# Shift-convolution taps: summed by accumulating transfers within SBUF instead of by matmuls

## The chip, the core and the metric

The kernel runs on one core of a Trainium2 chip. The metric is device time in microseconds of one execution; lower is better. The engines are PE (matrix products, with its weight loads shown as PEld), DVE and ACT (elementwise work), POOL (a slow elementwise engine that also issues DMAs) and SP (issues DMAs only). Data lies in HBM, in SBUF (128 partitions) and, for results of PE, in PSUM, which PE writes and DVE and ACT read.

## The reference

The sequence has S = 2048 positions and D = 640 channels, and all arrays are bf16. Two branches are mixed by a gate that is computed per position.

```python
# branch A: short convolution of k (4 taps), times v, then a long convolution by FFT
k_pad = jnp.pad(k, ((0, 0), (ks - 1, 0), (0, 0)))
for t in range(ks):                       # ks = 4
    k_shift = k_shift + k_pad[:, t:t + S, :] * shift_k[:, ks - 1 - t][None, None, :]
kv = k_shift * v
y = irfft(rfft(pad(kv)) * rfft(pad(ssm_k)))[:, :S, :]   # along the sequence
y = y + kv * ssm_D
a = q * y
# branch B: a two-layer MLP along the sequence
h = layernorm(x)                          # x is q
u = gelu(einsum("bsd,sf->bdf", h, w1) + b1)             # F = 1536
b = transpose(einsum("bdf,fs->bds", u, w2) + b2)
out = g * a + (1 - g) * b                 # g = sigmoid(sum(x * gate_w))
```

Only the loop over the four taps and the product with v are touched by the change.

## The kernel before

**Branch A.** The sequence is cut into P = 4 parts of 512 positions, and each part into NB = 4 tiles of 128 positions, so that there are 16 k tiles. `kv_load` loads a tile into `k4` (128 x 4 x 640: for each position the row itself and the three rows before it, 640 KB) and its v into `v_` (160 KB). There are four k4 buffers and five v buffers. `kv_tile` multiplies k4 by the broadcast tap weights `shkb` on DVE (one instruction of 2560 elements). It then sums the four products on PE: four matmuls with the identity (for the first two tiles of a part) or with a flip matrix that reverses the 128 positions (for the other two) are accumulated in PSUM, each in two halves of 320 columns, since a bank of PSUM holds no more. ACT copies the sum into a row of `kvb`, and DVE multiplies it by v. For the flipped tiles, v is turned first, by two more matmuls and a copy on ACT.

When the four tiles of a part are there, `a_split` forms sums and differences `es` of the halves of `kvb` (DVE), `a_freq` transforms them into the spectrum `A{j}` by matmuls with tables (PE, then copies on ACT). The filter goes through the same steps into `W{i}`, with sums and differences between neighbouring parts (`w_comb`). `pair(j, m)` multiplies A{j} with W{m-j} and adds it to `Z{m}`, on DVE; there are ten pairs and two Z buffers. `inverse(m)` transforms Z back on PE, and `epilogue(m)` turns half of the result with flip matmuls, multiplies by q, adds the MLP's output and stores.

**Branch B.** DVE computes the layernorm into `h` (bn_stats, then one instruction per tile). The first layer is 384 matmuls `pp<-h,w`, whose weights come in w1 loads, mostly issued by POOL; the second is 384 matmuls `pp<-gT,w`, whose weights come in w2 loads by POOL. ACT applies the gelu and moves the second layer's results to `o1`.

**What sets the order.** While the program is built, `_Plan.run` puts all operations in an order by a list schedule. Each has a cost, a priority `pr` (lower goes first) and predecessors by the tiles that it reads and writes; its rank is the longest chain that follows it. A DMA takes its engine 0.5 us (SP) or 1.2 us (POOL), and then its bytes at `DMA_RATE` 0.30 MB/us on one common pipe, and 2.0 us more. This gives one fixed order per engine, and the engines then run in that order and wait on semaphores. So an instruction that waits holds up all that is behind it on its engine, and this holds for the DMAs that SP and POOL issue too.

**Names in the profile.** All matmuls have line L290, all of DVE's two-operand products L676, all ACT operations L718, and all DMA issues L258; so groups are told apart by their tiles. `k<-k,shkb` is the tap product, `pp<-k,ident` and `pp<-k,flip` are the matmuls that sum the taps, `kvb<-kvb,v` is the product with v, `pp<-v,flip` turns v, `es<-kvb` is the split, `tT<-A,W`, `Z<-A,W` and `Z<-Z,tT` are the pairs, `W<-W,W` is w_comb, `W<-W` are small copies within SBUF issued by SP, `xg<-xg,gwb` is the gate's product and `pp<-Z,TI` the inverse.

Of the kernel before, what the change touches and what calls it, by code (L numbers as in the profile page):

```python
# [11 lines left out]
ACT = mybir.ActivationFunctionType  # L12
ALU = mybir.AluOpType
# [4 lines left out]
class _Tracker:  # L18
# [227 lines left out]
    def dma(self, stream, out_ap, in_ap, semname, noncontig=False, accum=False):  # L246
        reads = [in_ap]
        writes = [out_ap]
        acc = self.pre(stream, reads, writes)
        engobj = self.eng[stream]  # L250
        sem = self.dma_sems[semname]
        if accum:
            ins = engobj.dma_start(out_ap, in_ap, accum_op=ALU.add)
        elif noncontig:
            with self.nc.allow_non_contiguous_dma(reason="tiny"):
                ins = engobj.dma_start(out_ap, in_ap)
        else:
            ins = engobj.dma_start(out_ap, in_ap)  # L258
        ins.then_inc(sem, 16)
        self.dma_cnt[semname] += 16  # L260
        v = self.dma_cnt[semname]
        self.dma_hist[(semname, v)] = dict(self.known[stream])
        src = ("dma", semname, v)
        for reg, mode in acc:
            self.add_record(reg, mode, src)
        return v
# [250 lines left out]
def _build(nc, A_q, A_k, A_v, A_shift_k, A_ssm_k, A_ssm_D, B_x, B_w1, B_b1, B_w2, B_b2, gate_w, out):  # L517
    Bsz, S, D = A_q.shape
    F = B_w1.shape[1]
    KS = A_shift_k.shape[1]  # L520
# [4 lines left out]
    NB = n // 128  # L525
# [7 lines left out]
    with ExitStack() as es:  # L533
# [3 lines left out]
        T = _Tracker(nc, clk)  # L537
# [5 lines left out]
        plan = _Plan(T, 4)  # L543
# [61 lines left out]
        KR = 4  # L605
# [3 lines left out]
        KVB = 1  # L609
# [31 lines left out]
        for name, shape, dtype, t0, t1 in spec:  # L641
            size = mybir.dt.size(dtype)
# [19 lines left out]
        def vop(eng, cost, f, reads, writes, pr, ps=(), after=()):  # L662
            def emit():
                rr = [a() if callable(a) else a for a in reads]
                T.op(eng, f, rr, writes)
            return plan.add(eng, cost, emit, [a for a in reads if not callable(a)], writes, pr, ps=ps, after=after)

        def nel(ap):
            k = 1
            for st, ct in list(ap.ap)[1:]:  # L670
                k *= ct
            return k

        def tt(out_, in0, in1, op, pr, eng="DVE"):
            c = 0.07 + nel(out_) / 1920.0 if eng == "DVE" else 0.3 + nel(out_) / 500.0
            return vop(eng, c, lambda e: e.tensor_tensor(out_, in0, in1, op), [in0, in1], [out_], pr)  # L676
# [19 lines left out]
        def act(out_, in_, func, pr, bias=None, scale=None, accum=None, ps=(), after=()):  # L696
            kw = {}
            rr = [in_]
            k = 0
            if bias is not None:  # L700
                kw["bias"] = bias
                if isinstance(bias, bass.AP):
                    rr.append(bias)
                    k += 1
            if scale is not None:
                kw["scale"] = scale
                if isinstance(scale, bass.AP):
                    rr.append(scale)
                    k += 1
            ww = [out_]  # L710
            if accum is not None:
                kw["accum_out"] = accum
                ww.append(accum)
            c = 0.17 + nel(out_) / 1150.0 + 0.09 * k + (0.2 if accum is not None else 0)

            def f(e):
                src = in_() if callable(in_) else in_
                return e.activation(out_, src, func, **kw)  # L718

            return vop("ACT", c, f, rr, ww, pr, ps=ps, after=after)  # L720

        def dma(out_ap, in_ap, semname, pr, stream="SP", noncontig=False):
            if semname not in T.dma_sems:
                T.add_dma_sem(semname, es.enter_context(nc.semaphore(f"d_{semname}")))
            tot = mybir.dt.size(out_ap.dtype)
            for st, ct in list(out_ap.ap):
                tot *= ct

            def emit():
                T.dma(stream, out_ap, in_ap, semname, noncontig=noncontig)  # L730

            return plan.add(stream, 1.2 if stream == "POOL" else 0.5, emit, [in_ap], [out_ap], pr, dma=max(tot, 20000) / 1e6)

        def pe(pslist, mms, pr, after=()):
            reads = []
            for (p_, c0, w_, lhsT, rhs, st, sp) in mms:
                reads.append(lhsT)
                reads.append(rhs)
            cost = sum(0.016 + m[2] * 0.000372 for m in mms)

            def emit():
                full = [(pp[p_.slot][:, c0:c0 + w_], lhsT, rhs, st, sp) for (p_, c0, w_, lhsT, rhs, st, sp) in mms]
                T.mm_part(full)

            return plan.add("PE", cost, emit, reads, [], pr, ps=pslist, after=after)

        def two(p_):
            return lambda: pp[p_.slot][:, :].rearrange("p (c f) -> p c f", c=2)[:, :, 0:HD]
# [4 lines left out]
        def h2(ap):  # L753
            return ap.rearrange("p (c f) -> p c f", c=2)

        b = bufs
# [94 lines left out]
        def dram(t, off, ap):  # L851
            return bass.AP(tensor=t.tensor, offset=t.offset + off, ap=ap)

        dma(b["gwb"][:, :], dram(gate_w, 0, [[0, 128], [1, D]]), "gw", 2.3)

        def rows(t, q):
            return dram(t, q * 256 * D, [[D, 128], [128 * D, 2], [1, D]])

        def w1_load(s_, pr):
            for hf in range(2):  # L860
                nm = f"w1_{(2 * s_ + hf) % 3}"
                step = 4 if s_ == 0 else 8
                for t0 in range(0, 8, step):
                    dma(b[nm][:, t0:t0 + step, :],
                        dram(B_w1, (8 * hf + t0) * 128 * F + s_ * FSET * 128, [[F, 128], [128 * F, step], [1, FSET * 128]]),
                        f"{nm}_{t0}" if s_ < 1 else f"{nm}_p", pr + 0.35 * (8 * hf + t0), stream="SP" if s_ < 1 else "POOL")
# [4 lines left out]
        def wnat_load(i, pr):  # L871
            dma(b[f"wnat{i}"][:, :, :], dram(A_ssm_k, i * n, [[S, 128], [128 * S, DC], [1, n]]),
                f"wnat{i}", pr)
# [10 lines left out]
        for gi, g in enumerate(groups):  # L884
            xs = b[f"xs{g[0] // 8}"][:, g[0] % 8:g[-1] % 8 + 1, :]
            gn = len(g)
            pr = 1.0 + g[0] * 0.08
# [19 lines left out]
        def halves(p_, pairs, st=True, sp=True):  # L907
            k = len(pairs)
            res = []
            for c in range(2):  # L910
                for i, (l_, r_) in enumerate(pairs):
                    res.append((p_, c * 512, HD, l_, r_[:, c * HD:(c + 1) * HD], st and i == 0, sp and i == k - 1))
            return res
# [3 lines left out]
        p_ = _PS()  # L917
# [4 lines left out]
        for j in range(KS):  # L922
            p_ = _PS()
# [63 lines left out]
        for s_ in range(1, NSET):  # L987
            w1_load(s_, 2.5 if s_ < 2 else 6.0 + 2 * s_)
            for fi in range(FSET):
                p_ = _PS(True)  # L990
# [36 lines left out]
        def kv_tile(t, pr):  # L1027
            k4 = b[f"k4_{t % KR}"]
            v_ = b[f"v_{t % VR}"][:, :]
            r_ = t % NB  # L1030
            mat = b["ident" if r_ < 2 else "flip"][:, :]
            kb = b[f"kvb{t // NB % KVB}"][:, r_ if r_ < 2 else 5 - r_, :]
            if r_ >= 2:
                p_ = _PS()
                pe([p_], halves(p_, [(mat, v_)]), 1.1)
                act(h2(v_), two(p_), ACT.Copy, 1, ps=[p_])
            tt(k4[:, :, :], k4[:, :, :], b["shkb"][:, :, :], ALU.mult, pr)
            p_ = _PS()
            pe([p_], halves(p_, [(mat, k4[:, j, :]) for j in range(KS)]), 1.1)
            act(h2(kb), two(p_), ACT.Copy, 1, ps=[p_])  # L1040
            tt(kb, kb, v_, ALU.mult, pr - 2)

        def a_freq(j, pr):
            A = b[f"A{j}"]
# [9 lines left out]
        def kv_two(i):  # L1054
            for t in range(NB * i, NB * i + NB):
                kv_load(t, 8.0 + t)
                kv_tile(t, 11.0 + 0.5 * t)
# [176 lines left out]
```

## Time and profile before

| what | value |
|---|---|
| median of three timed runs | 226.09 us (223.95 to 227.66) |
| span of the profiled execution | 222.4 us (the profile gives no other time for it) |
| PE busy | 202.8 us, of it the tap sums 18.7 us |
| DVE busy | 201.8 us, of it the tap products 23.4 us |
| ACT busy | 139.9 us |
| POOL busy | 41.5 us |
| DMA | 39.88 MB, mean 179 GB/s |

The span runs from the first to the last instruction. Busy time is the sum of an engine's instructions, without waits. In a group's line, the number after x is how many instructions there are, then follow their busy time in us and the mean ns of one, and then the time for which the engine was idle just before them, with what ended most of it. In a line of the timeline, the first number is the start in us, the second the duration, and the bracket the idle time before it. Matmuls overlap, so that a group's busy time is less than count times mean.

### The profile page before, as it was taken

Reading aid. Unit: us, or ns where it says so; the run is one execution under the profiler, and the core shown is the slowest. Engines: PE = TensorE matmul, PEld = TensorE weight load, DVE = VectorE, ACT = ScalarE, POOL = GpSimd, SP = SyncE. Lnnn points to the kernel's source line nnn. Section 1 sums busy time; section 2 is a strip of 40 time slices with the busy share of each in tenths; the row PEclk is TensorE's granted clock in tenths of the full one; section 3 lists DMA queues with packets and bytes.
Section 4 is the critical chain, followed back from the end, with each engine's and each line's share of the span. In section 5 each row is a group of like instructions: output and inputs, shape, how many; then the busy total and the mean of one; then the engine's idle time right before and its main releaser. Section 6 shows DMA issues by size and latency. Waiting matters only on the chain.

```text
span 222.4 us, 3751 instructions
## 1 busy us (share of the span) xinstructions
PE 202.8 (91%) x1481; PEld 141.1 (63%) x1481; DVE 201.8 (91%) x253; ACT 139.9 (63%) x221; POOL 41.5 (19%) x79
## 2 busy tenths in 40 slices
PE   0829799999998998999999999999999999999991
PEld 0725547567675774777777777667777777767651
DVE  3379999899988998999999999999999999999771
ACT  4899988997579869683746511799431845432251
POOL 8563330301131010015171010000101101110000
PEclk9988999999999999999999999999999999999997
DMA  6999996139915894899962114302065845286003
GB/s 180 359 325 349 235 298 244 43 109 304 347 41 146 297 391 160 287 295 294 288 181 58 36 16 140 119 3 59 0 202 169 244 116 180 83 253 200 0 3 118
DMA packets 22087, 39.88 MB, mean 179 GB/s; under 512 B 1715, under 2 KB 17205, under 8 KB 22069
## 3 DMA queue, kind: packets, MB, share of 16 engines
q1 hardware_dynamic: 18964, 28.10, 39.8%
q0 software_dynamic: 3104, 11.54, 17.9%
q8 instruction: 12, 0.20, 0.4%
q14 instruction: 7, 0.05, 0.1%
HBM read 36.35 MB, written 2.62 MB: 175 GB/s over the span
## 4 chain that ended last, share of the span: by engine, by line
PE 60%; DVE 22%; ACT 11%; DMA 5%; issue 1%; DVEq 0%; SPq 0%
PE pp L290 60%; DVE Z L676 10%; DVE tT L676 7%; DMA k<-in_A_k_dram 3%; ACT wT L718 2%; ACT W L718 2%; DMA wnat<-in_A_ssm_k_dram 2%; ACT L718 1%; DVE es L676 1%; DVE cg L676 1%; ACT kvb L718 1%; DVE kvb L676 1%; DVE k L676 1%; DVE xg L676 1%; ACT TFs L718 1%
## 5 line engine op out<-in xcount | busy, mean ns | idle before, releaser
L290 PE MATMUL pp<-h,w 128*128 128x320 bf16 x384 | 54.9, 299 | 0.0
L290 PE MATMUL pp<-gT,w 128*128 128x320 bf16 x384 | 53.1, 299 | 0.0
L676 DVE TENSOR_TENSOR tT<-A,W 128x640 bf16<-128x640 bf16 (+4 forms) x44 | 48.0, 1121 | 0.3
L676 DVE TENSOR_TENSOR Z<-Z,tT 128x2560 bf16<-128x2560 bf16 (+3 forms) x35 | 47.1, 1370 | 0.1
L290 PEld LDWEIGHTS pp<-gT,w 128*128 128x128 bf16 x384 | 37.5, 98 | 14.8 <-issue 0.3
L290 PEld LDWEIGHTS pp<-h,w 128*128 128x128 bf16 x384 | 37.5, 98 | 14.6
L258 POOL DMA_DIRECT2D w<-in_B_w_dram x18 | 17.3, 962 | 117.7 <-PE pp L290 117.1
L718 ACT ACTIVATE o<-pp,c,omg 128x640 bf16<-128x640 f32 x16 | 14.2, 884 | 31.4 <-PE pp L290 31.4
L676 DVE TENSOR_TENSOR k<-k,shkb 128x2560 bf16<-128x2560 bf16 x16 | 23.4, 1485 | 0.6 <-DMA k<-in_A_k_dram 0.5
L718 ACT ACTIVATE A<-pp 128x640 bf16<-128x640 f32 x32 | 20.0, 717 | 2.0 <-PE pp L290 2.0
L718 ACT ACTIVATE gT<-pp,bf 128x640 bf16<-128x640 f32 x12 | 9.5, 792 | 18.3 <-PE pp L290 18.2
L290 PE MATMUL pp<-Z,TI 128*128 128x320 bf16 x128 | 18.4, 299 | 1.1 <-ACT kvb L718 1.1
L718 ACT ACTIVATE W<-pp 128x640 bf16<-128x640 f32 x24 | 15.9, 707 | 3.9 <-PE pp L290 3.8
L290 PE MATMUL pp<-ident,wnat 128*128 128x128 bf16 x80 | 8.0, 274 | 10.1 <-DMA wnat<-in_A_ssm_k_dram 5.4
L290 PEld LDWEIGHTS pp<-Z,TI 128*128 128x128 bf16 x128 | 12.4, 98 | 6.4 <-ACT kvb L718 1.4
L718 ACT ACTIVATE kvb<-pp 128x640 bf16<-128x640 f32 x16 | 11.2, 701 | 5.8 <-PE pp L290 5.8
L290 PEld LDWEIGHTS pp<-ident,wnat 128*128 128x128 bf16 x80 | 6.6, 124 | 11.2 <-DMA wnat<-in_A_ssm_k_dram 5.8
L893 DVE BATCH_NORM_STATS2 stats<-xs 128x6 f32<-128x320 bf16 x32 | 13.3, 475 | 0.0
L718 ACT ACTIVATE xg<-xg 128x640 bf16<-128x640 bf16 x16 | 11.6, 734 | 1.7 <-DVE xg L676 1.7
L676 DVE TENSOR_TENSOR Z<-A,W 128x5120 bf16<-128x5120 bf16 x4 | 11.3, 2819 | 0.7 <-ACT A L718 0.7
L290 PE MATMUL pp<-wT,TFc 128*128 128x320 bf16 x48 | 10.1, 300 | 1.7 <-ACT W L718 1.7
L290 PE MATMUL pp<-es,AFs 128*128 128x320 bf16 x64 | 10.1, 300 | 0.8 <-ACT gT L718 0.8
(92 smaller groups left out, 279.2 us busy)
## 6 DMA issues: line engine op xcount, KB each, us to landing
k<-in_A_k_dram SPq DMA_DIRECT2D x15, 640.0 KB, 7.7
w<-in_B_w_dram POOLq DMA_DIRECT2D x8, 768.0 KB, 5.8
w<-in_B_w_dram POOLq DMA_DIRECT2D x10, 512.0 KB, 6.1
wnat<-in_A_ssm_k_dram SPq DMA_DIRECT2D x4, 640.0 KB, 6.5
v<-in_A_v_dram SPq DMA_DIRECT2D x16, 160.0 KB, 7.4
xg<-in_A_q_dram SPq DMA_DIRECT2D x8, 320.0 KB, 7.1
xe<-in_A_q_dram SPq DMA_DIRECT2D x8, 320.0 KB, 3.1
out_dram<-cg SPq DMA_DIRECT2D x8, 320.0 KB, 4.3
```

Of the source, the lines that this page charges most:

```text
L258: ins = engobj.dma_start(out_ap, in_ap)
L290: ins = self.nc.tensor.matmul(ps_ap, lhsT=lhsT, rhs=rhs, start=start, stop=stop)
L676: return vop(eng, c, lambda e: e.tensor_tensor(out_, in0, in1, op), [in0, in1], [out_], pr)
L718: return e.activation(out_, src, func, **kw)
L893: vop("DVE", 0.41, (lambda o_, i_: lambda e: e.bn_stats(o_, i_))(o_, i_), [i_], [o_], pr)
```

## The change

The four tap products are no longer summed on PE. Two DMAs within SBUF, issued by POOL, add to what lies at their destination: the first adds the products of taps 2 and 3 to those of taps 0 and 1 (128 rows of 1280 elements, 320 KB), the second adds the second half of that sum to the first (640 elements, 160 KB). Both have the same semaphore, and the second waits for the first. DVE multiplies the sum by v. For the first two tiles of a part this product goes straight to `kvb`; for the other two it goes to the v buffer, is turned by two flip matmuls, and is copied to `kvb` by ACT. So v itself is no longer turned. In the planner, an accumulating DMA counts 2.5 times its bytes. The DMA call caps one row of a transfer at 2560 bytes.

```diff
         if accum:
-            ins = engobj.dma_start(out_ap, in_ap, accum_op=ALU.add)
+            ins = engobj.dma_start(out_ap, in_ap, accum_op=ALU.add, max_dma_last_dim=2560)
...
-        def dma(out_ap, in_ap, semname, pr, stream="SP", noncontig=False):
+        def dma(out_ap, in_ap, semname, pr, stream="SP", noncontig=False, accum=False):
...
-                T.dma(stream, out_ap, in_ap, semname, noncontig=noncontig)
-
-            return plan.add(stream, 1.2 if stream == "POOL" else 0.5, emit, [in_ap], [out_ap], pr, dma=max(tot, 20000) / 1e6)
+                T.dma(stream, out_ap, in_ap, semname, noncontig=noncontig, accum=accum)
+
+            size = max(tot, 20000) / 1e6 * (2.5 if accum else 1.0)
+            return plan.add(stream, 1.2 if stream == "POOL" else 0.5, emit, [in_ap], [out_ap], pr, dma=size)
...
-            mat = b["ident" if r_ < 2 else "flip"][:, :]
-            kb = b[f"kvb{t // NB % KVB}"][:, r_ if r_ < 2 else 5 - r_, :]
-            if r_ >= 2:
+            tt(k4[:, :, :], k4[:, :, :], b["shkb"][:, :, :], ALU.mult, pr)
+            nm = f"ka_{t % KR}"
+            dma(k4[:, 0:2, :].rearrange("p j d -> p (j d)"), k4[:, 2:4, :].rearrange("p j d -> p (j d)"),
+                nm, pr, stream="POOL", accum=True)
+            dma(k4[:, 0, :], k4[:, 1, :], nm, pr, stream="POOL", accum=True)
+            if r_ < 2:
+                tt(b[f"kvb{t // NB % KVB}"][:, r_, :], k4[:, 0, :], v_, ALU.mult, pr - 2)
+            else:
+                kb = b[f"kvb{t // NB % KVB}"][:, 5 - r_, :]
+                tt(v_, k4[:, 0, :], v_, ALU.mult, pr - 2)
                 p_ = _PS()
-                pe([p_], halves(p_, [(mat, v_)]), 1.1)
-                act(h2(v_), two(p_), ACT.Copy, 1, ps=[p_])
-            tt(k4[:, :, :], k4[:, :, :], b["shkb"][:, :, :], ALU.mult, pr)
-            p_ = _PS()
-            pe([p_], halves(p_, [(mat, k4[:, j, :]) for j in range(KS)]), 1.1)
-            act(h2(kb), two(p_), ACT.Copy, 1, ps=[p_])
-            tt(kb, kb, v_, ALU.mult, pr - 2)
+                pe([p_], halves(p_, [(b["flip"][:, :], v_)]), 1.1)
+                act(h2(kb), two(p_), ACT.Copy, 1, ps=[p_])
```

## The prediction

> **What bounds the kernel now.** I read the busy times first.
>
> ```profile
> PE 202.8 (91%) x1481; PEld 141.1 (63%) x1481; DVE 201.8 (91%) x253; ACT 139.9 (63%) x221; POOL 41.5 (19%) x79
> ```
>
> Two engines are level: PE at 202.8 us and DVE at 201.8 us of a span of 222.4 us. The chain that ended last gives PE 60% and DVE 22%, but a chain names only one of two engines that are never idle. So the stretches of 20 us (columns: sum, then PE, PEld, DVE, ACT, POOL busy, clock, DMA share, GB/s):
>
> ```profile
> 0.00:20.00 20.00, 9.91 (x93) 7.97 (x94) 11.16 (x30) 16.40 (x25) 12.95 (x41) 0.91 0.96 297
> ...
> 40.00:60.00 20.00, 19.31 (x138) 12.63 (x136) 19.16 (x21) 15.50 (x25) 3.06 (x6) 1.00 0.60 201
> 60.00:80.00 20.00, 19.22 (x142) 13.51 (x140) 18.23 (x18) 17.15 (x31) 3.09 (x5) 1.00 0.61 193
> ...
> 180.00:200.00 20.00, 20.00 (x149) 14.23 (x148) 19.86 (x19) 8.11 (x10) 3.05 (x3) 1.00 0.50 147
> 200.00:222.40 22.40, 17.54 (x127) 11.86 (x124) 15.50 (x28) 6.36 (x8) 0.00 (x0) 0.95 0.26 80
> ```
>
> DVE idles 8.8 us in the first 20 us (before any k tile), some 4 us from 20 to 100, 0.5 us from 100 to 200, and 6.9 us in the last stretch, of which 2.6 us is the output's way home after DVE's last instruction. DVE's work does not shrink here, so whatever PE loses, little more than the late gaps can be won. The end of DVE's timeline shows those:
>
> ```profile
> 209.11 0.88 DVE L676 TENSOR_TENSOR Z<-Z,tT 128x640 bf16<-128x640 bf16 x2
> 212.34 1.55 DVE L1151 CAST pb<-pp 128x640 bf16<-128x640 f32 x2 [2.35 <-PE pp L290]
> ...
> 218.95 0.83 DVE L676 TENSOR_TENSOR cg<-cg,o 128x1280 bf16<-128x1280 bf16 x1 [1.86 <-ACT o L718]
> ```
>
> Both waits come from PE: its backlog of second-layer matmuls (24 run from 205.55, 24 more from 214.50) stands between the last Z product and the end.
>
> **What goes.** These groups go or shrink:
>
> ```profile
> L290 PE MATMUL pp<-k,ident 128*128 128x320 bf16 x64 | 9.4, 299 | 0.0
> L290 PE MATMUL pp<-k,flip 128*128 128x320 bf16 x64 | 9.3, 299 | 0.0
> L718 ACT ACTIVATE kvb<-pp 128x640 bf16<-128x640 f32 x16 | 11.2, 701 | 5.8 <-PE pp L290 5.8
> L718 ACT ACTIVATE v<-pp 128x640 bf16<-128x640 f32 x8 | 5.4, 704 | 0.9 <-PE pp L290 0.8
> ```
>
> PE loses all 128 tap matmuls, 9.4 + 9.3 = 18.7 us; the 16 flip matmuls stay, on the product. ACT loses 24 - 8 = 16 copies of 0.70 us, 11.2 us; ACT is 63% busy, so I count it as nothing. PE's 18.7 us lie beside DVE's work and are worth only what DVE waited for PE at the end. With no backlog, only the last group of inverse matmuls follows the last Z: some 8 x 0.137 = 1.1 us plus its 0.3 us way in place of 2.35 us, a gain of 1.2 us; the last o is early, a gain of 1.86 us. Together **-3.0 us** (bounds 0 and -4.2, both waits whole). What is late next is DVE itself.
>
> DVE keeps 16 tap products of 1.485 us and 16 products with v of 0.486 us: zero change.
>
> **What is added.** 32 accumulating transfers on POOL, two per tile: 320 KB, then 160 KB, the second waiting for the first, and the v product for the second. No such transfer is in the trace. POOL's own plain transfers set the lower bound: when the DMA engines are quiet, 512 KB land in 4.6 to 4.8 us and 768 KB in 5.5 to 5.8 us. That is 0.9 us per 256 KB and 2.9 us fixed (about 1.0 of it issue, as the DMA issues of w last 962 ns). Plain, 320 KB would take 4.0 us and 160 KB 3.4 us: 7.4 us per tile. The other end is the only copy within SBUF, in traffic:
>
> ```profile
> W<-W SPq DMA_DIRECT2D x4, 160.0 KB, 7.9
> ```
>
> Two such are 15.8 us, and 320 KB would add 0.6. An add must also read its destination, so I charge twice the plain bytes (the planner's factor is 2.5): 5.1 + 4.0 = 9.1 us, nearer the POOL rows, since POOL issues them. The Trainium skill bears this out for another pattern: "Collectives: The Full Stack", section "The bandwidth ceiling", says an add on the way costs a second source read, not ALU time; no row here shows it. By "DMA: Bandwidth & Descriptors", "Anatomy of one DMA", 2.0 us plus bytes over 436 GB/s, a tile would take an estimated 5.2 us, below even my plain rows (a 512 KB load would be 3.2 us; the trace has 4.6), so the measurement stands.
>
> POOL's issue time grows by 32 x 0.96 = 31 us. It is 19% busy, but **in order**. While it stands on a second transfer, what is queued behind are the next tiles' transfers, the memsets of W, and the w loads, for which PE's first layer waits. In reverse, transfers stand behind a w load that waits for PE (11.0 and 16.2 us before those at 79.56 and 96.59). SP's k loads of tile t+4 now wait for the v product, not PE, as there are four k4 buffers.
>
> **Where it lands on the path: the first group.** DVE's timeline:
>
> ```profile
> 41.94 5.69 DVE L676 TENSOR_TENSOR k<-k,shkb 128x2560 bf16<-128x2560 bf16 x4
> 47.54 1.48 DVE L676 TENSOR_TENSOR W<-W,W 128x2560 bf16<-128x2560 bf16 x1
> ...
> 56.76 1.56 DVE L676 TENSOR_TENSOR es<-kvb 128x1280 bf16<-128x1280 bf16 x2
> ...
> 63.34 2.82 DVE L676 TENSOR_TENSOR Z<-A,W 128x5120 bf16<-128x5120 bf16 x1 [0.75 <-ACT A L718]
> ```
>
> Four tap products end at 43.4 to 47.5 us; today es ends at 58.3 and the first spectral product starts 5.0 us later. Until then DVE has only preparatory work, afterwards plenty (a pair with j = 0 is some 9 us, with j > 0 some 12 us). The DMA engines are empty from 42 to 47.5, so the eight transfers of the group run one after another: 4 x 480 KB = 1920 KB at 0.9 us per 256 KB, 6.8 us plain, doubled 13.5 us. From 44.5 that is 58.0; with 1.9 us to report, the last lands at 59.9. Then v product 0.5, flip 0.6, copy 0.7 and es 1.6 end at 63.3: **5.0 us late**. The first Z starts at 68.3.
>
> What fills? From 47.5: three w_combs 4.5, two gate products 1.6, so work lasts until 53.6. The k4 buffers come free only from about 54, and a k load takes 5.6 us or more, so the products of tiles 4 to 7 (5.9 us) no longer stand here but behind 60. Between 53.6 and 61 only four v products (1.9) remain: 5.5 us idle, less 0.75 us idle today, **+4.7 us**. If the planner moves the k products ahead of the statistics, or transfers cost the plain 6.8 us, this falls to zero; at the upper prices the last es ends 16.4 - 9.1 = 7.3 us later still, +12.
>
> **The later groups.** The second Z buffer lets DVE go on with pairs of A0: 9 + 9 us, then some 9 more, besides tap products and gate products, so A1 is not needed before about 100. Today es of group 1 ends at 78.2; two transfers and a reload later it is some 86. Covered. What I cannot see is each v product standing in DVE's order when its transfer is late: 12 tiles at 0 to 1 us. DMA shares of 0.6 to 0.8 between 40 and 120 leave no wide room for 16 x 480 KB doubled (54 us), so I take **+1.5 us**, bounds 0 and +12.
>
> **Sum:** -3.0 + 4.7 + 1.5 = +3.2 us, a span of 225.6. The page gives no time for the profiled execution apart from its span; the median of the timed runs, 226.1, is 3.7 us above it. I predict 225.6 + 3.7 = **229.3 us**, 1.4% above the median.
>
> **Rivals.**
> (a) *The transfers hide and PE's relief shows.* For it: empty DMA engines at 42 to 47.5, and a planner that reorders by the longer chain. Then -3.0, and DVE's waits for ACT's kvb and A in the middle (0.8 + 0.7) go as well: -4.5, or with the whole end -5.7; span 217.3, **221 us**. Against: k tiles 1 to 3 land only at 35 to 38 us, so tap products cannot move far.
> (b) *The transfers' chain becomes the bound*, the slower side: at the price of W<-W, 16.4 us per tile, the first group costs +12 and the in-order waits some +6: -3 + 18 = +15, **241 us**. It decides where a tile's two transfers take more than some 11 us, what DVE has to do in between. For: DMA shares near 1.0 at 56 to 60 and 80 to 84 us. Against: those are k loads, which now come later.
> (c) *Adds are far dearer for the DMA engines* (say four times the plain bytes): 16 x 480 KB are then 108 us, on top of the 63 us that the DMA shares of today's stretches from 40 to 160 amount to. The last group would land near 42 + 171 = 213, and some 30 us of pairs and end follow it: 243 + 3.7, **about 247 us**.
>
> **Chances.** Forecast 0.48 (half of it, +0 to +4.5 us, within 2%; the rest above), (a) 0.27 (0.16 faster by over 2%, 0.11 within), (b) 0.21, (c) 0.04. The 2% (4.5 us) is about what a measurement here tells from no change, as the runs differ by 1.6%. Faster 0.16; within 0.24 + 0.11 = 0.35; slower 0.24 + 0.25 = 0.49. The range goes from (a)'s 220.5 to (b)'s 241; the forecast's own is 226 to 234.
>
> **What would show it.** Right: no pp<-k matmuls, PE near 184 us, DVE still near 202 us with its new idle time between 50 and 68, ended by a k transfer; first Z<-A at 66 to 70; the 2.35 and 1.86 us waits at the end gone or short. Wrong: DVE idle before the pairs unchanged (then a), waits on k spread over all groups and PE waiting for w (then b), transfers landing in over 8 us each with DMA shares near 1 (then b or c). I would also be wrong if the planner puts the new work in an order that leaves DVE without pairs late, which no row of before shows.

## The result, and the profile after

| | before | after |
|---|---|---|
| median | 225.09 us (223.95 to 227.66, 4 runs) | 239.96 us (239.74 to 240.66, 4 runs) |
| ratio | 1 | 1.065 [1.059, 1.072] |
| span of the profiled execution | 222.4 us | 237.0 us (its own time: 240.18) |
| DVE idle within the span | 20.6 us | 35.2 us |
| PE idle within the span | 19.6 us | 44.9 us |

Ratios in this document leave out runs that took over 1.5% more than the fastest of the same kernel, so they need not be the quotient of the two medians.

The change costs 14.6 us of span. The page's busy times of the changed kernel:

```profile
PE 192.1 (81%) x1353; PEld 129.8 (55%) x1353; DVE 201.8 (85%) x253; ACT 130.1 (55%) x205; POOL 71.6 (30%) x111
```

PE lost 10.7 us of busy time and DVE not a tenth of a microsecond, so the whole 14.6 us is idle time of DVE (35.2 - 20.6). Where it lies is seen in the stretches of 20 us of the changed kernel (columns as before: sum, then PE, PEld, DVE, ACT, POOL busy, clock, DMA share, GB/s). The second block has two stretches of the kernel before:

```profile
0.00:20.00 20.00, 8.34 (x72) 5.96 (x72) 9.62 (x19) 14.61 (x22) 12.31 (x35) 1.00 0.89 255
...
40.00:60.00 20.00, 19.71 (x142) 13.18 (x141) 19.70 (x43) 16.84 (x32) 7.75 (x14) 1.00 0.73 198
60.00:80.00 20.00, 19.69 (x145) 13.67 (x143) 17.11 (x15) 13.38 (x23) 7.76 (x10) 1.00 0.97 267
80.00:100.00 20.00, 20.00 (x149) 14.23 (x147) 17.10 (x18) 9.72 (x19) 8.22 (x9) 1.00 1.01 301
100.00:120.00 20.00, 20.00 (x148) 13.86 (x146) 14.36 (x13) 12.39 (x21) 7.21 (x9) 1.00 0.82 215
120.00:140.00 20.00, 4.28 (x18) 1.73 (x15) 20.00 (x18) 5.07 (x7) 3.40 (x4) 0.65 0.91 242
140.00:160.00 20.00, 12.14 (x54) 7.09 (x55) 19.93 (x16) 6.61 (x10) 6.51 (x7) 0.67 0.68 146
...
200.00:220.00 20.00, 18.97 (x140) 13.48 (x139) 18.90 (x32) 7.34 (x9) 2.03 (x2) 1.00 0.65 195
220.00:240.00 20.00, 12.14 (x87) 7.97 (x84) 6.38 (x10) 5.47 (x7) 0.00 (x0) 0.88 0.10 34
```

```profile
80.00:100.00 20.00, 18.86 (x138) 12.81 (x137) 18.97 (x19) 15.63 (x30) 1.32 (x2) 1.00 0.81 270
100.00:120.00 20.00, 20.00 (x149) 14.41 (x148) 19.79 (x19) 10.41 (x19) 8.86 (x9) 1.00 0.70 214
```

Against the same stretches of before, DVE's idle time grew by 1.5 us in the first 20 us, by nothing from 20 to 60 (it fell by 0.3 us), by 8.4 us from 60 to 120 (11.4 instead of 3.0), by 0.1 us from 120 to 200, and by 4.8 us from 200 to the end (11.7 instead of 6.9). A second thing stands beside it: between 120 and 160 PE has little to do. DVE is busy there, so this costs nothing on the spot, but PE's second layer is now late.

**From 60 to 120: a group is late.** DVE's timeline (start, duration, in brackets the idle time before it):

```profile
56.44 1.48 DVE L676 TENSOR_TENSOR k<-k,shkb 128x2560 bf16<-128x2560 bf16 x1
...
66.81 1.56 DVE L676 TENSOR_TENSOR es<-kvb 128x1280 bf16<-128x1280 bf16 x2 [2.32 <-ACT kvb L718]
...
81.60 0.48 DVE L676 TENSOR_TENSOR kvb<-k,v 128x640 bf16<-128x640 bf16 x1
...
99.70 0.83 DVE L676 TENSOR_TENSOR xg<-xg,gwb 128x1280 bf16<-128x1280 bf16 x1 [2.51 <-DMA xg<-in_A_q_dram]
...
104.99 1.56 DVE L676 TENSOR_TENSOR es<-kvb 128x1280 bf16<-128x1280 bf16 x2 [4.07 <-ACT kvb L718]
...
109.50 2.83 DVE L676 TENSOR_TENSOR tT<-A,W 128x5120 bf16<-128x5120 bf16 x1 [1.54 <-ACT A L718]
...
139.61 1.55 DVE L676 TENSOR_TENSOR es<-kvb 128x1280 bf16<-128x1280 bf16 x2
...
169.01 1.55 DVE L676 TENSOR_TENSOR es<-kvb 128x1280 bf16<-128x1280 bf16 x2
```

The first and the third line are one tile (tile 4): its tap product starts at 56.44, its product with v at 81.60, 25 us later. The splits es of the four groups start at 66.8, 105.0, 139.6 and 169.0; before they started at 56.8, 76.6, 97.7 and 146.7:

```profile
76.60 1.56 DVE L676 TENSOR_TENSOR es<-kvb 128x1280 bf16<-128x1280 bf16 x2
...
97.69 1.56 DVE L676 TENSOR_TENSOR es<-kvb 128x1280 bf16<-128x1280 bf16 x2
...
146.70 1.55 DVE L676 TENSOR_TENSOR es<-kvb 128x1280 bf16<-128x1280 bf16 x2
```

The brackets are the idle time: es waits for the flipped rows of kvb, tT for the spectrum of this same group. The 2.51 us are another thing, a wait for a load of q that the gate needs; why that load is late was not looked into.

Why 25 us? Where POOL stands meanwhile (POOL's timeline; L253 are the accumulating transfers, L258 the plain loads):

```profile
58.22 0.87 POOL L253 DMA_DIRECT2D k<-k  x1 [0.38 <-DVE k L676]
...
61.75 0.93 POOL L258 DMA_DIRECT2D w<-in_B_w_dram  x1 [2.64 <-PE pp L290]
64.38 0.87 POOL L253 DMA_DIRECT2D k<-k  x1 [1.69 <-DVE k L676]
66.37 0.93 POOL L258 DMA_DIRECT2D w<-in_B_w_dram  x1 [1.12 <-PE pp L290]
67.28 0.91 POOL L253 DMA_DIRECT2D k<-k  x1
```

Tile 4's first transfer is issued at 58.22 and lands at 65.9. The second is issued only at 67.28, since a w load that waits for PE stands ahead of it in POOL's order, and lands at 76.4. DVE takes the sum up at 81.60, where the planned order has it. The DMA issues (number, KB each, median us from issue to landing):

```profile
k<-k POOLq DMA_DIRECT2D x16, 320.0 KB, 7.1
...
k<-k POOLq DMA_DIRECT2D x16, 160.0 KB, 5.9
...
W<-W SPq DMA_DIRECT2D x4, 160.0 KB, 3.1
```

Over the twelve tiles of the later groups, 17 to 27 us lie between the start of a tap product and that of its product with v, 22.3 us as a mean: the tap product itself 1.5 us, 0.6 us until POOL issues the first transfer, 6.8 + 6.4 us of landings (the medians over all tiles are the 7.1 and 5.9 above), 2.5 us until POOL issues the second, and 4.6 us that the sum lies ready before DVE's order comes to it.

**From 120 to the end: PE starves, then has a backlog.** PE's timeline:

```profile
116.21 4.51 PE L290 MATMUL pp<-h,w 128*128 128x320 bf16 x32
130.93 0.71 PE L290 MATMUL pp<-v,flip 128*128 128x320 bf16 x2 [10.21 <-DVE v L676]
...
140.48 4.45 PE L290 MATMUL pp<-es,AFc 128*128 128x320 bf16 x16 [2.76 <-DVE es L676]
...
156.38 5.24 PE L290 MATMUL pp<-gT,w 128*128 128x320 bf16 x24 [7.38 <-DMA w<-in_B_w_dram]
```

The first layer is done at 120.7. The second layer's weights use SBUF that the k tiles held, and the last tap product now runs at 146.7 (before at 101.0), so the first of these loads is issued at 149.06 (before at 102.8). From 156.4 PE is busy, with gaps of 1 us at most, to 232.5, and DVE's end waits for it in the two places that my prediction wanted to see shrink:

```profile
223.68 1.55 DVE L1154 CAST pb<-pp 128x640 bf16<-128x640 f32 x2 [2.80 <-PE pp L290]
...
233.55 0.83 DVE L676 TENSOR_TENSOR cg<-cg,o 128x1280 bf16<-128x1280 bf16 x1 [5.12 <-ACT o L718]
```

2.80 and 5.12 us, where before they were 2.35 and 1.86.

### The profile page after: what moved, and what is told of

It reads as the page before. It is cut to its first block, busy times and chain, and to the rows that moved or that the text cites. A ratio compares the mean times of both kernels' runs of the same rounds, so it can differ in the third digit from the quotient of the medians.

```text
span 237.0 us, 3505 instructions
## 1 busy us (share of the span) xinstructions
PE 192.1 (81%) x1353; PEld 129.8 (55%) x1353; DVE 201.8 (85%) x253; ACT 130.1 (55%) x205; POOL 71.6 (30%) x111
## 3 DMA queue, kind: packets, MB, share of 16 engines
q0 software_dynamic: 7712, 19.40, 35.2%
## 4 chain that ended last, share of the span: by engine, by line
PE 60%; DVE 14%; DMA 10%; ACT 9%; issue 4%; POOL 1%; SPq 0%; POOLq 0%; DVEq 0%
PE pp L290 60%; DMA w<-in_B_w_dram 6%; DVE tT L676 4%; DMA wnat<-in_A_ssm_k_dram 4%; DVE Z L676 4%; ACT wT L718 3%; DVE k L676 2%; ACT W L718 2%; DVE es L676 1%; DVE cg L676 1%; ACT A L718 1%; ACT o L718 1%; POOL k L694 1%; ACT AFs L718 1%; ACT AFc L718 1%
## 5 line engine op out<-in xcount | busy, mean ns | idle before, releaser
L290 PE MATMUL pp<-gT,w 128*128 128x320 bf16 x384 | 55.6, 305 | 9.2 <-DMA w<-in_B_w_dram 8.1
L290 PE MATMUL pp<-h,w 128*128 128x320 bf16 x384 | 53.8, 299 | 0.0
L290 PEld LDWEIGHTS pp<-gT,w 128*128 128x128 bf16 x384 | 38.0, 100 | 25.7 <-issue 8.7
L290 PEld LDWEIGHTS pp<-h,w 128*128 128x128 bf16 x384 | 37.5, 98 | 14.6
L253 POOL DMA_DIRECT2D k<-k x32 | 29.0, 966 | 43.7 <-DVE k L676 23.0
L258 POOL DMA_DIRECT2D w<-in_B_w_dram x18 | 18.4, 1025 | 75.5 <-PE pp L290 73.2
L676 DVE TENSOR_TENSOR k<-k,shkb 128x2560 bf16<-128x2560 bf16 x16 | 23.6, 1481 | 6.6 <-DMA k<-in_A_k_dram 6.6
L290 PE MATMUL pp<-Z,TI 128*128 128x320 bf16 x128 | 19.9, 310 | 0.0
L718 ACT ACTIVATE xg<-xg 128x640 bf16<-128x640 bf16 x16 | 11.7, 733 | 6.9 <-DVE xg L676 6.9
L290 PE MATMUL pp<-ident,wnat 128*128 128x128 bf16 x80 | 7.5, 254 | 9.6 <-DMA wnat<-in_A_ssm_k_dram 8.6
L290 PE MATMUL pp<-v,flip 128*128 128x320 bf16 x16 | 4.0, 339 | 13.4 <-DVE v L676 13.4
L718 ACT ACTIVATE kvb<-pp 128x640 bf16<-128x640 f32 x8 | 5.6, 700 | 16.3 <-PE pp L290 16.3
L290 PE MATMUL pp<-es,AFc 128*128 128x320 bf16 x64 | 11.6, 342 | 3.1 <-DVE es L676 3.1
```

What stands on the lines that cost most here:

```text
L253: ins = engobj.dma_start(out_ap, in_ap, accum_op=ALU.add, max_dma_last_dim=2560)
L290: ins = self.nc.tensor.matmul(ps_ap, lhsT=lhsT, rhs=rhs, start=start, stop=stop)
```

## The experiments

**The theories.** X: the landings of the two transfers in each tile's chain (with only four k4 buffers, so that the next load of a buffer waits for the product with v) set the pace of the groups, and all else follows. P: it is the planner's price of 2.5 for an accumulating transfer, which asks for each sum later than it is there. W: it is PE's starving, since the second layer's weights wait for SBUF. S: it is the start, where SP now issues the first k loads ahead of the filter's.

### The planner's price: price1

```diff
-            size = max(tot, 20000) / 1e6 * (2.5 if accum else 1.0)
+            size = max(tot, 20000) / 1e6 * (1.0 if accum else 1.0)
```

> Every instruction and transfer stays; only the planner's price of an accumulating DMA goes from 2.5 to 1.0 times its bytes, and with it the order on each engine. Theory P (the order made by a price that is too high stretches the tap stage, and the last tap product at 148 us holds back the second layer's weights): the last tap product comes near 125 us, the first w2 load near 128, PE idles under 12 us between 110 and 160 instead of 28, and the time is 222 to 230 us. Theory X (the transfers themselves, 7.1 + 5.9 us to landing under load, and four k4 buffers set the pace): the tap stage ends as late as now whatever the order, 236 to 242 us, now with DVE waiting for k transfers.

Measured: 237.04 us, ratio 1.052 [1.046, 1.057]; span 234.2. The last split starts at 156.4 instead of 169.0, the w2 loads go out at 138 and 140, and the slack is gone. POOL's waits (total, how often, longest) show what stands there now:

```profile
POOL k L253 <- DMA k<-k: 34.6, 10, 6.1
```

In the changed kernel this sum is 13.5 us. P is worth some 3 us of the 14; the rest stays with an order that asks for each sum as soon as it lands.

### The second layer's weights: w2apart

```diff
-            buf(f"w2_{i}", [128, FT, 256], BF16, 91, END)
+            buf(f"w2_{i}", [128, FT, 256], BF16, 83, END)
```

The second layer's weights lie over the first layer's weight buffers now, not over the k tiles.

> The two w2 buffers are laid over the w1 buffers instead of over shkb and k4. Theory W (what costs is that the second layer's weights wait for the last tap product): the first w2 load comes at 120 to 135 us instead of 149, PE's idle time between 120 and 156 falls by 10 us or more, 228 to 234 us. If instead DVE's own waits between 60 and 120 us make up the loss: within 2 us of the changed kernel's 240.

Measured: 240.64 us, 1.066 [1.061, 1.070]. The w2 loads go out at 126 and 130 instead of 149, and nothing is won: PE still stands 14.4 us for DVE's v, and at the end DVE waits 7.8 us for PE at pb. PE idles 15.2 us from 120 to 160 instead of 23.6, and the time is the same, so W as stated falls. The edit is not clean, though: the order changed with it, and the last two splits start at 145.4 and 179.2, later than in the changed kernel (139.6 and 169.0). That PE starves because the groups are late, and does not make them late, fits this, but is not shown by it.

### The relief alone: no_xfer

```diff
-            nm = f"ka_{t % KR}"
-            dma(k4[:, 0:2, :].rearrange("p j d -> p (j d)"), k4[:, 2:4, :].rearrange("p j d -> p (j d)"),
-                nm, pr, stream="POOL", accum=True)
-            dma(k4[:, 0, :], k4[:, 1, :], nm, pr, stream="POOL", accum=True)
```

> The 32 transfers are left out, so that the four taps are not summed (the product with v takes the first tap's product alone). All else of the change stays: this is PE's and ACT's relief alone. If the relief is worth what the prediction's step says (-3.0, at most -4.2 and some middle waits): 219 to 223 us. If PE's tap sums cost the kernel nothing: 224 to 227 us. What lies between this and 240 us is the transfers' cost.

Measured: 225.47 us, 0.998 [0.995, 1.001]. This is the most useful number of the study: all of PE's and ACT's relief, with no transfer to pay for, is worth nothing in the order that the planner makes of it. DVE's idle time is 20.6 us as before, but it lies elsewhere. First the end of this kernel's timeline of PE, then two places in that of DVE:

```profile
205.96 2.29 PE L290 MATMUL pp<-Z,TI 128*128 128x320 bf16 x8 [8.02 <-DVE Z L676]
208.95 6.14 PE L290 MATMUL pp<-Z,TI 128*128 128x320 bf16 x24 [0.70 <-DVE Z L676]
```

```profile
127.82 2.82 DVE L676 TENSOR_TENSOR Z<-A,W 128x5120 bf16<-128x5120 bf16 x1 [0.63 <-PE pp L290]
132.71 2.82 DVE L676 TENSOR_TENSOR Z<-A,W 128x5120 bf16<-128x5120 bf16 x1 [2.07 <-PE pp L290]
...
211.97 0.88 DVE L676 TENSOR_TENSOR Z<-Z,tT 128x640 bf16<-128x640 bf16 x2
214.59 1.56 DVE L1150 CAST pb<-pp 128x640 bf16<-128x640 f32 x2 [1.74 <-PE pp L290]
```

The backlog is gone, and PE now waits 8.0 us for DVE. The end is shorter, nearly as forecast: the wait for the last o is gone, that for PE at pb is 1.74 us instead of 2.35, and from the start of DVE's last Z products to the end of its work 8.1 us pass instead of 10.7. But DVE comes to these products 2.9 us later than before (211.97 instead of 209.11). Of this, 2.7 us are the two new waits: DVE is ahead here, and the next pairs wait for PE's inverse matmuls, which end at 127.78 and 132.68. Before, DVE idled 0.1 us from 120 to 140. A smaller thing is the clock: with the gap, the granted clock is 0.66 from 200 to 220, and 24 inverse matmuls take 6.14 us, where before 28 took 4.03 us at full clock. It can have cost no more here than a part of the 1.74 us that DVE still waits. By the Trainium skill, "TensorE: Matmul & The Clock Gate", Part 1, an idle window of some 3.4 us sets the clock to half rate until work has gone on for about as long; the trace agrees in kind (0.66 as a mean of a stretch with an 8.0 us gap). So all of the loss in the changed kernel is what the transfers cost, with the order that comes with them.

### Half the tiles: tiles01_p1

```diff
+        XF = [0, 1, 4, 5, 8, 9, 12, 13]
+            if t in XF:    # these by transfers, the others by matmuls as in the kernel before; price 1.0
```

> Only tiles 0 and 1 of each part, which need no turning, use transfers (16 transfers), tiles 2 and 3 are summed on PE as before; price 1.0. Theory P: half the relief (9.4 us of PE) with transfers covered by the other two tiles: 219 to 225 us. Theory X: two of four buffers still take a round through both transfers, 228 to 235 us.

Measured: 226.11 us, 1.002 [0.999, 1.005]. With two tiles of each part summed by transfers the splits start at 59.0, 79.9, 98.4 and 143.7, no later than 3.3 us after those of before, and the time is that of before. DVE's first 20 us are as poor as in price1 (6.36 us busy in both, 11.16 before), and that costs nothing here.

### The start order: start, price1_start, tiles01_start

```diff
-                kv_load(t, 8.0 + t)
+                kv_load(t, 16.0 + t)
```

This gives the filter's loads their old place ahead of the k loads; price1_start and tiles01_start do the same on top of price1 and tiles01_p1.

> The changed kernel with the k loads' priority number raised by 8, so that SP issues the filter's and x's loads first again, as before the change (the changed kernel issues five k loads ahead of the first wnat load, whose transposes start at 13.4 us instead of 5.4). Theory S (the longer chain pulls the k loads forward and starves the beginning): DVE's idle time in the first 20 us falls from 10.4 to about 9 us, PE starts near 5.5 us, 236 to 238.5 us. If the beginning is not on the path: 239 to 241 us.

> Price 1.0 and the k loads behind the filter's and x's loads. Price 1.0 alone has 237.0 us and DVE idle 13.6 us in the first 20 us, against 8.8 before the change. Theory S: that idle time falls to about 9 and the time by some 4 us, to 231 to 234 us; what is left above 225.5 is then the transfers' landing time in a ring of four buffers. If the tap stage alone sets the pace, the gain at the start is lost again: 235.5 to 238 us.

> Half of the tiles by transfers, price 1.0, and the k loads behind the others. The same without the last step is 226.1 us and has DVE idle 13.6 us in the first 20 us. Theory S: 221 to 223.5 us, faster than before the change. If DVE's time lost at the start comes back as waits for k later: 224.5 to 227 us.

Measured: start 246.65 us, 1.104 [1.091, 1.116]; price1_start 239.65 us, 1.068 [1.050, 1.086]; tiles01_start 228.6 us, 1.014 [0.990, 1.038]. S falls, and for the changed kernel on the wrong side: the early k loads were a help. In start, DVE is busy for 13.24 us only from 20 to 40 (19.05 in the changed kernel), waits 9.4 us for k loads, and the splits of parts 2 and 3 get no earlier (142.6 and 169.8). The other two are not apart from the same kernels without this step (1.052 and 1.002): their intervals overlap.

### Copies instead of adds: copy

```diff
-            ins = engobj.dma_start(out_ap, in_ap, accum_op=ALU.add, max_dma_last_dim=2560)
+            ins = engobj.dma_start(out_ap, in_ap)
```

> The changed kernel with plain copies in the place of the 32 accumulating transfers: same order, same bytes written, same waits; the taps are not summed. If reading the destination and adding costs the transfers what the prediction charged (twice the plain bytes): 320 KB land in 1.1 us less, 160 KB in 0.6 us less, and the time falls by 2 to 4 us to 236 to 238. If an add costs what a copy costs: 239 to 241 us, and the landing times stay at 7.1 and 5.9 us.

Measured: 238.47 us, 1.065 [1.051, 1.079], which lies between the two forecasts and is not apart from the changed kernel. The DMA issues of this kernel:

```profile
k<-k POOLq DMA_DIRECT2D x16, 320.0 KB, 5.9
...
k<-k POOLq DMA_DIRECT2D x16, 160.0 KB, 5.3
```

An add lands 1.2 and 0.6 us later than a copy; its issue on POOL is also 0.36 us longer (median 906 ns against 548). In the kernel's time this does not appear, and the fixed order hides it: with the planner's price of 2.5 the sum lies ready for 6.6 us with copies (4.6 with adds), and POOL issues the second transfer 3.7 us after the first has landed (2.5), so that a tap product and its product with v stand 22.6 us apart (22.3; means of the later twelve tiles). So at this price the adding costs nothing that the run can show; two transfers without any adding cost as much. What an add costs at price 1.0, where the sum is taken as it lands, was not tried.

### The first group and the later ones apart: g0 and g123

```diff
-        XF = [0, 1, 4, 5, 8, 9, 12, 13]
+        XF = [0, 1, 2, 3]               # g0; price 2.5
+        XF = list(range(4, 16))         # g123; price 2.5
```

> Only the four tiles of the first part are summed by transfers (price 2.5 as in the changed kernel); the other twelve keep their matmuls. My prediction's step (first group +4.7 us, later ones next to nothing): some 230 us, ratio 1.02. Theory X (the ring of later groups is what costs; in the trace of the changed kernel DVE's idle time from 20 to 60 us hardly grew): within 2 us of before, 225 to 228, ratio 0.995 to 1.01, although the first Z product still starts some 5 us late or more.

> The first part keeps its matmuls; parts 1 to 3 (tiles 4 to 15) are summed by transfers at price 2.5. Theory X (later groups carry the cost, each tile's buffer is held until two transfers have landed): 235 to 240 us, ratio 1.045 to 1.065, with es of parts 1 to 3 late by over 10 us. My prediction's step (later groups covered, +1.5 us): 226 to 228 us.

Measured: g0 230.96 us, 1.026 [1.020, 1.031], which is +5.8 us; g123 236.63 us, 1.049 [1.042, 1.056], which is some +11 us. So the first group alone is dearer than X had it, and in sum about as dear as my prediction had it. DVE's timeline of g0 reads like the prediction's paragraph:

```profile
43.15 5.69 DVE L676 TENSOR_TENSOR k<-k,shkb 128x2560 bf16<-128x2560 bf16 x4
...
57.86 3.02 DVE L676 TENSOR_TENSOR W<-W,W 128x2560 bf16<-128x2560 bf16 x2 [3.09 <-ACT W L718]
...
71.70 1.56 DVE L676 TENSOR_TENSOR es<-kvb 128x1280 bf16<-128x1280 bf16 x2 [5.58 <-ACT kvb L718]
...
76.68 2.82 DVE L676 TENSOR_TENSOR Z<-A,W 128x5120 bf16<-128x5120 bf16 x1 [2.01 <-ACT A L718]
```

The four tap products stand together as in the kernel before, and DVE idles 12.3 us from 40 to 80 (2.6 before). That is 9.7 us more, twice the forecast; some 4 us come back elsewhere, 2.6 of them after 200 us, where PE's backlog is gone. In the changed kernel it idles 3.2 us there: with every tile on the longer chain, the planner put the tap products at 11.7 (two), 31.8 and 35.6 us, and the layernorm's statistics and `h` fill the landings. So the first group's price is real, and the changed kernel doesn't pay it there. The later groups alone cost most of the loss. Both prices together (some 17 us) are more than the 14.6 us of all tiles; the three kernels have different orders, so that the two prices need not add up.

### One transfer per tile: one_xfer and one_xfer25

```diff
-            dma(k4[:, 0, :], k4[:, 1, :], nm, pr, stream="POOL", accum=True)
```

The first has price 1.0, the second 2.5.

> Price 1.0, with the second transfer of each tile left out (the lower half of the sum is then missing from the output), so that a tile waits for one landing, not for two. Theory X, time in proportion to the landing time in each tile's chain (7.7 of 14.2 us remain): 225.5 + 0.54 x 11.5 = 231.7 us, range 229 to 234, ratio 1.02 to 1.035. Rival T (a threshold: up to some landing time the ring hides all): within 2 us of before. Rival Q (what costs is POOL's queue, in that any transfer stands behind w loads that wait for PE): over 234 us.

> Only the first transfer, as before, but with the planner's price of 2.5 instead of 1.0, so that the fixed order asks for each v product later; the transfers themselves are the same. Theory O (a late order costs by itself once the last split is later than some 147 us, where A3 is first needed): 231 to 236 us, ratio 1.025 to 1.045, with the last es after 147. Rival T (only the landings count): 226 to 229 us, as at price 1.0.

Measured: one_xfer 227.33 us, 1.011 [1.007, 1.015]; one_xfer25 231.11 us, 1.025 [1.018, 1.032]. The first lies below X's range and just above T's 2 us: the cost is not in proportion to the landings, and it is far below Q's 234 us. The splits of one_xfer (DVE's timeline):

```profile
59.46 1.55 DVE L676 TENSOR_TENSOR es<-kvb 128x1280 bf16<-128x1280 bf16 x2
82.36 1.56 DVE L676 TENSOR_TENSOR es<-kvb 128x1280 bf16<-128x1280 bf16 x2
108.53 1.56 DVE L676 TENSOR_TENSOR es<-kvb 128x1280 bf16<-128x1280 bf16 x2
137.11 1.55 DVE L676 TENSOR_TENSOR es<-kvb 128x1280 bf16<-128x1280 bf16 x2
```

They follow each other by 23 to 29 us. Parts 1 and 2 are 6 and 11 us later than before, yet the last split is earlier than before's 146.7, because before it simply had time until then. This is the cover that my prediction counted on, and with one landing it is nearly enough. With two the changed kernel's groups follow each other by 29 to 38 us and the last is at 169.0. one_xfer25, with the same transfer and only the later order, has its splits at 134.5 and 155.7 for parts 2 and 3 and loses some 3 us to one_xfer (1.025 against 1.011): a late order costs by itself, as much here as between price1 and the changed kernel (1.052 against 1.065).

### The second hand-over against its bytes: small2

```diff
-            dma(k4[:, 0, :], k4[:, 1, :], nm, pr, stream="POOL", accum=True)
+            dma(k4[:, 0, 0:256], k4[:, 1, 0:256], nm, pr, stream="POOL", accum=True)
```

> Price 1.0, both transfers, but the second adds 256 of the 640 columns only (64 KB in place of 160 KB; the rest of that addition is missing from the output). Theory H (a second hand-over costs, whatever it moves: issue on POOL behind the first landing, and a fixed landing time): the second transfer still lands in 5 us or more, and the time stays near that of both transfers at price 1.0, 233 to 238 us, ratio 1.035 to 1.055. Rival B (the bytes cost): the time falls to near that of one transfer alone, 227 to 230 us, ratio 1.01 to 1.02.

Measured: 234.71 us, 1.041 [1.035, 1.047]. The profiled execution of this kernel took 237.17 us, more than its other runs, so of its trace I use the landings only:

```profile
k<-k POOLq DMA_DIRECT2D x16, 320.0 KB, 6.4
k<-k POOLq DMA_DIRECT2D x16, 64.0 KB, 5.5
```

A transfer of 64 KB lands in 5.5 us, one of 160 KB in 6.5 us (price1). With 60% of its bytes gone, the second hand-over still costs three quarters of what it cost: 1.041 - 1.011 = 0.030 against 1.052 - 1.011 = 0.041. H holds, B falls.

### The runs side by side

| transfers per tile | price | ratio | es of parts 2 and 3 start at |
|---|---|---|---|
| none (no_xfer) | | 0.998 | 84, 123 |
| matmuls (before) | | 1 | 98, 147 |
| two, on half of the tiles | 1.0 | 1.002 | 98, 144 |
| one | 1.0 | 1.011 | 109, 137 |
| one | 2.5 | 1.025 | 134, 156 |
| two, the second of 64 KB | 1.0 | 1.041 | (not used) |
| two | 1.0 | 1.052 | 129, 156 |
| two | 2.5 | 1.065 | 140, 169 |

Read downwards: PE's relief 0, the first hand-over +1.1%, the second +4.1% (+3.0% with 40% of its bytes), the late order +1.3%. No version with transfers beat the kernel before, and where the relief is worth nothing none can.

**What stays open.** one_xfer25 and price1 have their splits at nearly the same times and differ by 6 us, so the splits' times are not the whole price. What differs in the traces is POOL: in price1 it stands 34.6 us on first transfers before it may issue second ones. How the 9 us of the second hand-over divide between POOL's order, DVE's and the four k4 buffers is not settled. A fifth k4 buffer would tell; it wasn't tried. The wait for PE's inverse matmuls that took back the relief in no_xfer stands in one_xfer too (3.90 us, before the Z product at 131.24), so its 1.1% need not be all landings.

## Why the prediction was wrong

I forecast 229.3 us; it is 240.0 us. (The 3.7 us that I added from span to median were too many: most runs on record show 1.8.) The time lies within the range, at the place of rival (b), 241 us. Step by step:

- **"Together -3.0 us" for the end: measured 0 over the whole kernel** (no_xfer, 0.998 [0.995, 1.001]). The stated lower bound 0 was right. At the end itself the step holds, 2.6 us in no_xfer. I took the two late waits away, asked what is late next, and answered "DVE itself". What I had at nothing is that a DVE that gets ahead must wait for PE in the middle: 2.7 us at two Z products. In the changed kernel both late waits even grew, to 2.80 and 5.12 us, because PE's second layer starts later. PE's busy time fell to 192.1 us, not to 184: with the gaps, its granted clock is 0.65 and 0.67 from 120 to 160, and 16 matmuls of the spectrum take 4.45 us there (2.34 us at full clock, at 106.23).
- **"First group +4.7 us": the mechanism holds where it occurs, the size by luck** (g0: +5.8 us [4.6, 6.9]). es starts much later than worked out (71.7 instead of 61.7), since the flip matmuls of the products with v stand behind first-layer matmuls on PE: the products start at 63.76 and 64.90, their flips at 67.57 and 70.02. DVE's idle time from 40 to 80 grows by 9.7 us, and gains elsewhere bring the sum back near 4.7. In the changed kernel the term is 0.6 us between 40 and 80, plus 1.5 us at the start: I had named the case ("if the planner moves the k products ahead of the statistics, ... this falls to zero") and not taken it.
- **"The later groups. ... Covered", +1.5 us: this step failed.** g123 puts it at some +11 us [9.5, 12.5]; in the changed kernel it is most of the 8.4 us from 60 to 120 (7.3 of them after 80, of which 2.5 are the wait for q) and, through PE's late second layer, the 4.8 us at the end. I put es of group 1 at "some 86"; it is at 105. The argument that A1 isn't needed before 100 was sound, but I let the chain of one turn grow by two landings once, and it grows in every turn of four buffers: 105, 140, 169.
- **"5.1 + 4.0 = 9.1 us" per tile: mis-sized.** Measured: 7.1 + 5.9 = 13.0 us of landings, and 2.5 us between them on POOL. The surcharge for adding was right: 1.7 us charged ("An add must also read its destination"), 1.8 us measured against copies (1.2 and 0.6). What was wrong is the plain price under it, 7.4 us; copies take 5.9 + 5.3 = 11.2 us in these places. The 7.4 came from quiet rows of POOL's loads, and the quietest 320 KB transfers do land in 3.6 and 3.7 us here (at 142.86 and 148.52); most of the others run in stretches with DMA shares of 0.7 to 1.1. The row that I had put aside, W<-W at 7.9 us in traffic, gave 16.4 us; the 13.0 lie midway. By the Trainium skill, "Collectives: The Full Stack", "The bandwidth ceiling", an add in a ring step costs a second source read; the runs show 1.2 us of 7.1 and 0.6 of 5.9 for the add, and not what it is spent on.
- **Rival (b) had the cause**, with its condition as stated: it "decides where a tile's two transfers take more than some 11 us". They take 13.0 us, 15.5 with POOL's part. Its sum (-3 + 12 + 6) is near the result by luck, for its terms are not: the relief is 0, the first group is nearly hidden, and the later groups cost twice its 6 us. **(c)** is out: landings are near those of copies. **(a)** would need the transfers to hide; that is nearly so with one per tile, and so with two on half of the tiles, and even then the relief is worth nothing. (Two roundings are 0.1 us off, and nothing hangs on them: (a)'s lower end comes to 220.4 us by its terms, and the estimate of 5.2 us per tile to 5.1.)

## What to carry to other kernels

Work moved off an engine that is level with another can be worth nothing, as the 18.7 us here: price the relief by leaving the work out, not by its busy time. A chain of small transfers inside a ring of buffers costs by its number of landings more than by its bytes, in every turn of the ring, so count landings per turn and take their time from rows of the same stretch, with its traffic. And a planner's price is part of the change: an order that asks for data late costs as surely as data that come late.

## What the hardware showed that I had not expected

- A dependent transfer of 64 KB within SBUF lands in 5.5 us (median, beside traffic); the same median is 4.4 to 6.5 us for 160 KB and 4.5 to 7.7 us for 320 KB, over the runs with accumulating transfers. The quietest two of 320 KB in the changed kernel landed in 3.6 and 3.7 us (DMA share 0.63 meanwhile, their own bytes included). W<-W, again 160 KB, took 7.9 us in the kernel before (DMA share 1.01 for three of the four) and 3.1 us in the changed one (two of the four in 2.1 and 2.3 us, at 0.57 and 0.75).
- Adding instead of copying costs 0.6 to 1.2 us of a landing, and at the planner's price of 2.5 no time that could be measured.
- PE's granted clock is 0.65 and 0.67 in the two stretches in which it has gaps (120 to 160), and 0.66 at the end of no_xfer, so its last matmuls get slower when PE is relieved late: 256 ns each (6.14 us / 24) instead of 144 ns (4.03 us / 28). It cost little there, as DVE's wait for them got shorter.
